# Rounding weights partly on ScalarE and doing the first batch's gated block in seven products, in an attention and SwiGLU kernel

## The chip, the core and the metric

The kernel runs on one core of one Trainium2 chip. The metric is the time of one execution on the device in microseconds (us), as the median of several. A profiled execution gives the span from the first to the last instruction, some 2 us less than that execution's time. A run of one core has no second core to compare with, so it counts as slow only where it is over 1.5% above the fastest of its kernel.

## The reference

Two blocks follow each other. Attention masks a score wherever the six hash bits of query and key differ; its output, put back as 3072 tokens of 512, goes through a gated feed-forward block.

```python
batch, n_heads, seq, head_dim = (4, 8, 768, 64)          # n_tokens 3072, d_model 512, d_ff 1536
q_bits = (np.einsum('bhsd,dk->bhsk', q, proj) > 0)       # k_bits likewise, 6 bits each
scores = np.where(mask, scale * q @ k^T, -1e9)           # mask: equal bits
attn = softmax(scores);  x = (attn @ v) as (3072, 512)
g = x @ w_gate;  silu = g * (1.0 / (1.0 + np.exp(-g)))
val = x @ w_val
return (silu * val @ w_out).astype(np.float32)
```

The three weight matrices are double precision. The kernel sees each double as two 32-bit words, loads them in 36 pieces of 128 x 512 doubles (512 KB each: 12 of gate, 12 of value, 12 of down weights), and rounds every piece to fp32 itself.

## The kernel before

Work on a pair of heads is cut into units: one half of the queries against one sixth of the keys, so 12 units a pair and 48 a batch. A half of a pair (six units) ends in a norm, whose first VectorE instruction is a reciprocal `r`. There is one such `r` for every six units, so its starts serve as a clock for the whole kernel.

The program order on each engine is the order in which this code issues instructions. Attention of batch one runs alone (there is nothing to multiply yet) while VectorE rounds weights. From batch two on, products of the feed-forward block of the batch before are put between the units of attention. Rounding takes seven VectorE operations a piece, in a loop of two buffers:

```python
wraw = ctx.enter_context(tc.tile_pool(name="wraw", bufs=2))
def narrow():
    for i, (w, _) in enumerate(pieces):
        t = words.pop(i)
        lo, hi = t[:, :, 0], t[:, :, 1]
        wi = w.bitcast(I32)
        nc.vector.tensor_scalar(wi, hi, scalar1=3, scalar2=0x3FFFFFFF, ...)       # shift, and
        yield True
        nc.vector.scalar_tensor_tensor(out=wi, in0=hi, scalar=-(1 << 30), ...)    # sign
        yield True
        ...                       # four more: top bits of lo, rounding bit, add, abs of hi
        nc.vector.scalar_tensor_tensor(out=w, in0=hi, scalar=float(897 << 20), in1=w, ...)
        load_words(i + 2)         # refills the buffer just read
        yield True
```

`narrow_on(n)` advances this generator by `n` yields. The feed-forward block of batch one is done with plain products; those of batches two to four with seven block products in place of eight (`up_strassen`, `down_strassen`), which need sums of weight blocks. After batch one's up block, those sums are formed and sent to DRAM, from where they come back group by group:

```python
if b == 0:
    up_plain(x); down_plain(out_of)
else:
    up_strassen(x, b, first); ... down_strassen(out_of)
```

```python
LATE = 2 * NP * 2 * NCH                 # two batches
for u in range(0, LATE, 2):             # two units at a time
    score(u); score(u + 1)              # TensorE scores, then ScalarE exponentials
    for x in left: attend(x)            # TensorE
    while due: norm(due.pop(0))
    for x in left: add(x)               # VectorE: acc, sums of exponentials
    ...
    if not atoms:                       # batch one: nothing to multiply
        narrow_on(3 if u % 12 == 6 else 2)
        continue
    credit += 5.5
    while atoms and credit >= atoms[0][0]:
        size, atom, _ = atoms.pop(0); credit -= size
        atom()                          # a product of the feed-forward block
        narrow_on(2 * size)
for u in range(LATE, N + NCH, NCH):     # batches three and four: six units at a time
    ...                                 # scores, norm, scores, attend, then 15.75 products
```

PSUM has three banks for products and sums, and two double ones for scores.

The softmax here doesn't subtract the row's maximum and nothing guards it: scores larger than these inputs give would overflow.

## Time and profile before

| | before |
|---|---|
| median (three runs) | 1076.83 us |
| profiled span, mean granted TensorE clock | 1073.6 us, 1.000 |
| `r` of batch one's last half | 119.08 us |
| `r` of batch two's last half | 379.98 us |
| that `r` to the end | 693.6 us |

The prediction shows the main lines of this profile. The rows show TensorE's busy share, in tenths, and its granted clock, in tenths of full speed, over 40 slices of the span.

```profile
PE   9999999999999999999999999999999999999998
PEclk9999999999999999999999999999999999999999
```

No slice has an idle TensorE or a lowered clock. The stretch from batch one's last `r` to batch two's last (start:end, length, then busy us and instructions of PE, PEld, DVE, ACT and POOL, granted clock, DMA share, GB/s) says the same of the part that the change rebuilds:

```profile
119.08:379.98 260.90, 257.21 (x998) 125.46 (x998) 223.69 (x377) 58.34 (x88) 41.16 (x68) 1.00 0.41 122
```

TensorE loses 3.7 of 260.9 us there with VectorE at 86%. ScalarE is at 22%, and nothing that it does there concerns the weights.

### The profile page before, as it was taken

The numbers are of one execution on the slowest core, as the hardware profiler recorded it, in microseconds if no ns is written. First come the engines' busy times: TensorE is split into PE (matmuls) and PEld (weight loads), VectorE is DVE, ScalarE is ACT, GpSimd is POOL, SyncE is SP. The second block draws the span as 40 slices with busy tenths as digits, with TensorE's granted clock in tenths as the row PEclk, the third lists the DMA queues.
The fourth block names the chain that finished last, engine by engine and source line by source line (L and its number), as shares of the span: only waits on it lengthen the run. The fifth ranks groups of instructions, "written<-read, shape, count | busy, mean of one in ns | idle before, by whom it ended". The sixth has DMA issues, their size and how long they took to land.

```text
span 1073.6 us, 11817 instructions
## 1 busy us (share of the span) xinstructions
PE 1059.8 (99%) x4537; PEld 589.1 (55%) x4537; DVE 731.9 (68%) x1209; ACT 280.0 (26%) x449; POOL 86.0 (8%) x169
## 2 busy tenths in 40 slices
PE   9999999999999999999999999999999999999998
PEld 4444454554543444455555667554545777555687
DVE  5888988999897564767667465675757554555632
ACT  5544322212222123223232222323333010111100
POOL 1000000000014400010000000000000000111000
PEclk9999999999999999999999999999999999999999
DMA  6333322413325832251512212241212100333101
GB/s 167 75 84 84 84 78 93 109 60 108 92 89 160 296 104 57 66 132 55 113 50 84 50 35 50 69 114 54 80 54 69 54 17 24 103 103 103 35 20 40
DMA packets 110328, 88.86 MB, mean 83 GB/s; under 512 B 86496, under 2 KB 95200, under 8 KB 110272
## 3 DMA queue, kind: packets, MB, share of 16 engines
q0 software_dynamic: 16416, 62.27, 18.5%
q1 hardware_dynamic: 93056, 25.64, 10.9%
q8 instruction: 36, 0.59, 0.2%
q10 hardware_dynamic: 800, 0.20, 0.1%
q14 instruction: 20, 0.16, 0.0%
HBM read 70.78 MB, written 17.30 MB: 82 GB/s over the span
## 4 chain that ended last, share of the span: by engine, by line
PE 92%; DVE 6%; DMA 1%; ACT 1%; issue 0%; ACTq 0%; DVEq 0%
PE up L511 30%; PE po L511 15%; PE sc L422 15%; PE av L433 12%; PE up L493 11%; PE po L614 4%; DVE r L461 2%; PE sum L458 2%; PE hps L360 2%; DVE acc L444 1%; DMA ram<-ws 1%; DVE xT L464 1%; PE hps L372 1%; DVE acc L448 1%; ACT A L424 0%; PE idle L137 0%
## 5 line engine op out<-in xcount | busy, mean ns | idle before, releaser
L511 PE MATMUL up<-xT,wup 128*128 128x384 f32 x576 | 205.5, 490 | 0.0
L422 PE MATMUL sc<-qT,kT 64*128 64x384 f32 x768 | 165.5, 509 | 4.5 <-ACT A L424 1.9
L424 ACT ACTIVATE A<-sc 128x768 f32<-128x768 f32 x160 | 128.9, 812 | 128.6 <-PE sc L422 89.9
L511 PE MATMUL up<-xc,wup 128*128 128x384 f32 x432 | 158.7, 490 | 2.5 <-DVE c L515 1.9
L511 PEld LDWEIGHTS up<-xT,wup 128*128 128x128 f32 x576 | 107.8, 190 | 81.3 <-DVE hid L515 3.9
L461 DVE RECIPROCAL r<-sum 128x384 f32<-128x384 f32 x32 | 81.8, 2558 | 93.4 <-PE sum L458 93.4
L493 PE MATMUL up<-xT,wup 128*128 128x384 f32 x384 | 130.4, 492 | 2.1 <-DVE hid L481 1.0
L448 DVE TENSOR_TENSOR acc<-acc,A 128x768 f32<-128x768 f32 x128 | 121.9, 952 | 3.3
L433 PE MATMUL av<-A,vraw 128*64 128x386 f32 x640 | 117.8, 497 | 0.0
L511 PEld LDWEIGHTS up<-xc,wup 128*128 128x128 f32 x432 | 80.5, 190 | 63.3 <-DVE c L515 9.9
L422 PEld LDWEIGHTS sc<-qT,kT 64*128 64x128 f32 x768 | 63.1, 186 | 78.0 <-issue 43.4
L493 PEld LDWEIGHTS up<-xT,wup 128*128 128x128 f32 x384 | 71.0, 190 | 60.7 <-issue 4.2
L515 DVE TENSOR_TENSOR c<-c,up 128x384 f32<-128x384 f32 x108 | 57.9, 550 | 55.8 <-PE up L511 55.4
L271 POOL DMA_DIRECT2D wup<-ram x72 | 38.6, 536 | 581.6 <-PE up L511 581.5
L515 DVE TENSOR_TENSOR hid<-hid,up 128x384 f32<-128x384 f32 x108 | 57.5, 548 | 39.6 <-PE up L511 39.1
L433 PEld LDWEIGHTS av<-A,vraw 128*64 128x64 f32 x640 | 40.2, 136 | 65.1 <-issue 65.1
L614 PE MATMUL po<-wo,hid 128*128 128x512 f32 x144 | 63.6, 596 | 0.0
L422 PE MATMUL sc<-qb,kb 64*128 64x384 bf16 x384 | 63.2, 323 | 0.0
L476 ACT ACTIVATE c<-up 128x384 f32<-128x384 f32 x42 | 20.6, 490 | 155.1 <-PE up L493 98.8
L511 PE MATMUL po<-wup,hid 128*128 128x256 f32 x216 | 50.0, 381 | 0.0
L511 PE MATMUL po<-wo,hid 128*128 128x256 f32 x216 | 49.7, 379 | 0.0
L511 PE MATMUL po<-wo,wup 128*128 128x256 f32 x216 | 49.6, 379 | 0.0
(108 smaller groups left out, 1002.1 us busy)
## 6 DMA issues: line engine op xcount, KB each, us to landing
wup<-ram POOLq DMA_DIRECT2D x36, 512.0 KB, 3.8
wup<-ram POOLq DMA_DIRECT2D x36, 384.0 KB, 3.4
vraw<-in_v_dram SPq DMA_DIRECT2D x16, 384.0 KB, 3.2
words<-in_moe_w_val_dram POOLq DMA_DIRECT2D x12, 512.0 KB, 3.9
words<-in_moe_w_out_dram POOLq DMA_DIRECT2D x12, 512.0 KB, 3.6
ram<-ws POOLq DMA_DIRECT2D x12, 512.0 KB, 4.6
words<-in_moe_w_gate_dram POOLq DMA_DIRECT2D x10, 512.0 KB, 3.9
qraw<-in_q_dram SPq DMA_DIRECT2D x48, 96.0 KB, 3.5
```

The source lines that it names most:

```text
L271: nc.gpsimd.dma_start(places[k % 2][:, PARTS[part], :], ram[k % NG][:, PARTS[part], :])
L360: nc.tensor.matmul(ps[:, 0:HQ], hash_w[name], T[name, n][:, half * HQ : (half + 1) * HQ], start=True, stop=True)
L422: nc.tensor.matmul(sc[:, h, 0:HQ], x["k", n][rows, ks], x["q", n][rows, qs], start=start, stop=not start)
L424: nc.scalar.activation(weights(u)[:, :, 0:HQ], sc[:, :, 0:HQ], AF.Exp, scale=SCALE)
L433: nc.tensor.matmul(ps[h * D : (h + 1) * D, 0:AW], raws["v", n][:, h, c, :], a[:, h, :], start=c == 0, stop=c == NCH - 1)
L448: nc.vector.tensor_tensor(acc[n, half], acc[n, half], a[:, :, 0:HQ], op=ALU.add)
L458: nc.tensor.matmul(ps[h * D : (h + 1) * D, 0:HQ], ones, t[:, h, :], start=True, stop=True)
L461: nc.vector.reciprocal(r, ps[:, 0:HQ])
L493: nc.tensor.matmul(ps, up_weight(w, f, j), x[j][:, halves[half]], start=j == 0, stop=j == NJ - 1)
L511: nc.tensor.matmul(ps, a, x, start=start and i == 0, stop=i == len(pairs_) - 1, skip_group_check=True)
L515: nc.vector.tensor_tensor(o, a, b, op=op)
L614: nc.tensor.matmul(ps, hidden(f, half)[:, i * P : (i + 1) * P], wo[:, f, :], start=f == 0, stop=f == NF - 1)
```

## The change

The intent is to spend less TensorE time in batch one's feed-forward block, by giving it seven products too. For that the weights must be rounded and their sums formed before batch one's attention ends, which VectorE alone can't do; so three of the operations per piece go to the lightly loaded ScalarE. The core of the diff, with cuts marked:

```diff
     def narrow(i):
+        nc.vector.tensor_single_scalar(w, w, FLOOR, op=ALU.max)
+        ahead = scalar_steps(i + 1)          # ScalarE's three, for the NEXT piece
+        for k in range(3):
+            if ahead:
+                ahead[k]()
             yield True
+            ...                              # VectorE: shift (k == 0), sign (k == 1)
         nc.vector.tensor_tensor(wi, wi, lo, op=ALU.add)
-        ...                                  # four of VectorE's seven are gone or changed
-            load_words(i + 2)
+        load_words(i)
         yield True
+    def scalar_steps(i):
+        return [lambda: nc.scalar.activation(lo.bitcast(FP32), top, AF.Identity, bias=whole, ...),
+                lambda: nc.scalar.activation(lo, lo.bitcast(FP32), AF.Identity, bias=unwhole),
+                lambda: nc.scalar.activation(w, hi.bitcast(FP32), AF.Abs)]
+    EARLY = 16
     def load_words(done, queue=nc.gpsimd):
+        for i in range(len(words), len(pieces)):
+            if i - done > (4 if i < EARLY else 2):
+                break
+            words[i] = (spare[i % 5] if i < EARLY else       # five buffers, in `hid`
+                        wraw.tile([P, PIECE, 2], I32, ...))  # two, from piece 16 on
...
+    def form(n, pair): ...                   # sums of an up group as soon as its pieces are rounded,
+                                             # straight to DRAM
...
-    LATE = 2 * NP * 2 * NCH
+    LATE = NP * 2 * NCH
-        narrow_on(3 if u % 12 == 6 else 2)
+        prepare_on(2 if u < 4 else 4)        # batch one
...
-        credit += 15.75
+        credit += 14 if n < 2 * NP else 15.75
             atom()
-            narrow_on(2 * size)
+            ahead += 1.4 * size
+            prepare_on(int(ahead))
+            ahead %= 1
...
-        if b == 0:
-            up_plain(x)
-            down_plain(out_of)
-        else:
-            up_strassen(x, b, first)
+        up_strassen(x, b, first)
```

The five early buffers lie in the tensor that holds the gated block's output, which is free until batch one's products begin. Batch two moves from the two-unit loop to the six-unit loop. The key's hash bits are now taken by ScalarE, too, with a short VectorE scaling behind.

## The prediction

> **What bounds the kernel now.** I read the busy shares, then the chain of waits, then stretches of time, then single instructions.
>
> ```profile
> PE 1059.8 (99%) x4537; PEld 589.1 (55%) x4537; DVE 731.9 (68%) x1209; ACT 280.0 (26%) x449; POOL 86.0 (8%) x169
> ...
> PE 92%; DVE 6%; DMA 1%; ACT 1%; issue 0%; ACTq 0%; DVEq 0%
> ```
>
> TensorE is busy for 99% of the span and is 92% of the chain that ended last. Removing matmul time therefore shortens the run one for one, unless a second engine is nearly full where it is removed. Stretches (start:end, length, then busy time of PE, PEld, DVE, ACT, POOL) show where that is so:
>
> ```profile
> 78.00:104.00 26.00, 25.36 (x150) 11.25 (x148) 23.10 (x31) 12.71 (x21) 1.06 (x2) 1.00 0.31 74
> 125.00:165.00 40.00, 40.00 (x162) 20.45 (x163) 36.04 (x61) 10.20 (x16) 3.17 (x6) 1.00 0.37 90
> 478.82:508.43 29.61, 29.61 (x131) 14.96 (x130) 20.14 (x32) 10.42 (x18) 2.15 (x4) 1.00 0.21 63
> 508.43:537.19 28.76, 28.76 (x123) 14.80 (x122) 19.10 (x30) 8.14 (x14) 2.14 (x4) 1.00 0.48 105
> ```
>
> While the weights are rounded (first two rows) VectorE is at 89 to 90%; later (last two) at 67%. So the early stage has two bounds almost level. Its chain shows VectorE in the loop: reciprocal, xT, acc, then the exponential that frees the next scores:
>
> ```profile
> 106.70 2.56 DVE r L461
> ...
> 109.32 0.62 DVE xT L464
> 109.94 0.88 DVE acc L444
> ...
> 110.92 0.82 ACT A L424
> ...
> 111.79 1.89 PE sc L422 x12
> ```
>
> The chain also gives the pace of each product (two records per matmul):
>
> ```profile
> 232.27 7.94 PE up L493 x24
> 368.10 7.92 PE po L614 x18
> 702.54 27.46 PE up L511 x84
> 865.91 18.33 PE po L511 x84
> ```
>
> Plain up: 7.94/12 = 0.662 us a matmul; plain down 7.92/9 = 0.88; seven-product up 27.46/42 = 0.654; seven-product down 18.33/42 = 0.436.
>
> **What the Trainium skill says.** "VectorE: DVE Perf Modes", "The perf-mode tier table", puts fp32 tensor_scalar at twice the rate of tensor_tensor. The trace agrees: 128x512 takes 421 ns as a tensor_scalar and 690 as a two-tensor form, so the two-source steps are the costly ones. "ScalarE: Activation LUTs", "What ACT_TABLE_LOAD costs", gives an ACTIVATE 186 ns + 0.833 ns per element and about 93 more for a pointer bias; the trace's 384-element sign with a pointer bias took 580 ns against 600. My estimate from it for the new 512-element ones is 0.71, 0.71 and 0.61 us, about 1.8 a piece when they overlap. "PSUM — Partial Sum Buffer", "Engine vs sequencer instructions", calls the ScalarE and VectorE queues strict FIFO: an instruction that waits holds up everything behind it. No line of this trace isolates that, but my third step rests on it. "DMA: Bandwidth & Descriptors", "Anatomy of one DMA — SWDGE (gpsimd) path", gives 2.0 us + bytes/436e3, 3.2 us for a 512 KB piece; here it is 3.6 to 3.9.
>
> **The change, part by part.**
>
> *TensorE.* Batch one's up block: 192 plain matmuls (127.1 us) become 12 x 7 x 2 = 168 (109.9): -17.2. Its down block: 72 x 0.88 = 63.4 becomes 126 x 0.436 = 54.9: -8.5. Pairs 5 to 7 hash with 32-column blocks instead of 0.745 us full matmuls: about -4 in all. Steps of six units switch less between products, and the wait on stores of the sums (7 times, 15.4 us of VectorE idle, PE only 48.44 of 50 us busy at 300 to 350 us) goes. I take the total from spans. In the old kernel the reciprocal of batch one's last half starts at 119.08 and that of batch two's last half at 379.98: 260.9 us. The new stage is eight steps of 14 units, as in the last two rows above: 4 x (29.61 + 28.76) = 233.5. The old rest (1073.6 - 379.98 = 693.6) still holds 27 plain down matmuls (23.8); the new has one chunk of 42 (18.3): 688.1. With nothing stretched: 119.1 + 233.5 + 688.1 = 1040.7, or -33.
>
> *First batch (attention alone), VectorE.* The period is 26.2 us per pair of heads (reciprocals 80.47 to 106.70). Old VectorE load per pair, by distances between starts: ten acc at about 0.95, two norms of 3.15, two bit evictions of 0.61, 13 rounding steps of 0.57: 24.4. New: acc and norms 15.8; one stage of weights, i.e. four pieces of four steps (0.455 + 0.455 + 0.61 + 0.69 = 2.2; max is single-source) = 8.8, and eight 128x256 sums at 0.4 = 3.2; two bf16 scalings of the key bits, estimated at 0.2 each. That is 28.2: VectorE becomes the bound. The first pair absorbs it, because VectorE idles 6.35 us at 20 to 27 us; the other three stretch by 2.2, 2.2 and 0.6 (the last has only half the sums), with some jitter: **+5.4**. ScalarE rises from 12.8 to about 21 of 28 us per pair; its words come four ahead, so I expect no stall from it.
>
> *Second batch, first six steps (84 product steps of TensorE, 29.2 us each step).* VectorE: 18.7 per step (last two rows above, less four evictions of 0.667 us that move to ScalarE), plus 1.4 x 14 = 19.6 preparation steps of about 0.5 = 9.9. That is 28.6 of 29.2, 98%, and not evenly spread: some 22 us of it falls in the 18.3 us of the products, while in the 10.9 us of scores it waits for sums. Three PSUM banks let it lag two or three products. Worked through by hand, counting from the end of a gate group's fifth product: VectorE, 0.8 late, frees the first bank at 2.2 us where TensorE could use it at 1.3 (0.9 lost); in the value group the same bank comes free at 11.5, wanted at 10.5 + 0.9 (0.1). About 1.1 us a step.
>
> *The same steps, ScalarE.* From piece 16 on, a piece's words are asked for two ahead only, after the last VectorE instruction of the piece that held the buffer. The instruction order puts the first ScalarE step on those words just behind the next max. The load takes about 0.5 + 3.8 us, one piece lasts 4/1.4 products = 3.7 us. So ScalarE stands at its queue's head waiting for the load, and the copy of p1 and the tanh behind it come late, and VectorE and the PSUM banks after them. The hand working again, for a step that only rounds, counting from its first scores: loads asked for at 10.8, 18.1 and 25.3 us land at 14.6, 21.8 and 29.0; the last holds the max of its piece to 30.8, the second holds a tanh to 22.9, and the last product ends at 31.3 where it would end at 29.2 alone; the next reciprocal is another 0.3 late. That is 2.4 in place of 1.1. Taking it for all six: 2.4 x 6 = **+14.4**.
>
> *Sum.* 1040.7 + 5.4 + 14.4 = 1060.5 of span; the timed median lies 3.2 over the profiled span (1076.83 - 1073.6): 1063.7. My hand working ignores that the rate 1.4 and the 14 units were surely chosen by someone who measured, so I shade it down to **1061 us**.
>
> **Rivals.**
> - *Pure TensorE gain*: stalls absorbed, about 1040.7 + 3.2 = 1044. For it: at 125 to 165 us TensorE lost nothing with VectorE at 90%. Against: the load sums of 28.2 against 26.2 and 28.6 against 29.2.
> - *VectorE or the load loop bounds the second batch fully*: 4 to 6 us per step, 1070 to 1083. For it: the arithmetic of 4.3 against 3.7 us. Against: the scores part of each step breaks the loop, and eight of the 20 preparation steps in steps two and three are sums that need no words.
> - *Bringing batch one's weights back from DRAM is late*: 12 more groups of 0.9 MB in about 175 us is some 60 GB/s over the 90 to 105 now, with loads of 3.4 to 3.8 us that have over 13 us of slack. I give it no time.
>
> **Range and chances.** The two stretches are the uncertainty: 1 to 10 us in the first, 4 to 27 in the second. That gives 1046 to 1075. Two per cent faster is 1055.3, some 6 us under my figure: chance 0.3. Slower by 2% needs 1098: 0.02. The rest, 0.68, is within 2%.
>
> **What would show it.** The 264 plain matmuls vanish, the seven-product ones rise from 504 + 378 to 672 + 504, and each keeps its pace. The reciprocal of batch one's last half comes at about 124.5, and VectorE is over 95% busy from 40 to 120 us. The six steps from there last about 31.6 each with ScalarE idle on "DMA words" and TensorE idle on VectorE; the later steps stay at 29. I am wrong if the six steps last 29 (then about 1047), if ScalarE delays exponentials in the first batch, or if VectorE's new instructions take other times than I gave them.

## The result, and the profile after

Ratios here are the mean time of one kernel's fast runs over that of the other's of the same rounds, so they are not quite the ratio of the medians quoted beside them.

| | before | after |
|---|---|---|
| median | 1076.82 us | 1104.47 us (1102.44 to 1105.51) |
| ratio, 95% interval | | 1.0256, 1.0238 to 1.0273 |
| profiled span, clock | 1073.6 us, 1.000 | 1103.7 us, 0.985 |
| `r` of batch one's last half | 119.08 | 128.04 |
| `r` of batch two's sixth step | | 358.30 |
| `r` of batch two's last half | 379.98 | 416.50 |
| that `r` to the end | 693.6 | 687.2 |

The changed kernel is 2.6% slower; 1061 us and the whole range were wrong. The page after, with the busy line, the slices and the chain of waits:

```profile
PE 1049.9 (95%) x4597; PEld 601.9 (55%) x4597; DVE 714.1 (65%) x1230; ACT 387.1 (35%) x629; POOL 99.5 (9%) x192
...
PE   8999888888888999999999999999999999999998
...
PEclk9999898999999999999999999999999999999999
...
PE 76%; DVE 13%; ACT 4%; DMA 4%; issue 3%; POOL 0%; DVEq 0%; POOLq 0%; ACTq 0%
```

TensorE's share of the chain fell from 92 to 76%, VectorE's rose from 6 to 13%, and ScalarE and DMA have 4% each. The loss has a place: from the fifth slice to the thirteenth TensorE is at 8 tenths, that is from some 110 to 359 us (a slice is 1103.7/40 = 27.6 us), and the clock falls below nine tenths in two of these slices. After that both rows are as before. So are the paces of the products, here in the chain:

```profile
547.24 27.50 PE up L535 x84
...
867.81 18.33 PE po L535 x84
```

Before, 84 records of the same two kinds took 27.46 and 18.33 us. The stretches, from one `r` to the next, first a pair of batch one and then the six steps of batch two:

```profile
71.35:99.66 28.31, 26.07 (x150) 11.12 (x148) 27.33 (x43) 21.56 (x35) 8.95 (x14) 1.00 0.73 221
```

```profile
128.04:166.91 38.87, 33.02 (x120) 16.11 (x120) 31.60 (x57) 14.33 (x23) 4.51 (x8) 0.90 0.47 126
166.91:203.85 36.94, 33.24 (x128) 15.68 (x128) 27.58 (x52) 16.62 (x27) 7.95 (x13) 0.91 0.42 135
203.85:240.85 37.00, 31.14 (x120) 15.18 (x120) 27.04 (x49) 14.07 (x22) 8.07 (x13) 0.95 0.60 173
240.85:281.59 40.74, 33.50 (x128) 15.87 (x128) 28.78 (x52) 22.74 (x36) 4.77 (x9) 0.92 0.33 108
281.59:325.18 43.59, 33.34 (x122) 15.76 (x124) 28.55 (x50) 19.73 (x31) 4.25 (x8) 0.92 0.48 129
325.18:358.30 33.12, 30.32 (x130) 14.79 (x132) 27.17 (x47) 12.81 (x21) 2.30 (x6) 1.00 0.19 56
```

In the first batch VectorE is busy for 27.33 of 28.31 us, just as told. The six steps take 230.3 us together where the prediction had 189.5. VectorE is at 66 to 82% in them, so its average does not bound them; TensorE has 35.7 us of idle time (230.3 less the sum 194.6 of its busy column) and is itself slower, at a clock of 0.90 to 0.95 in the first five. Who waits for what, from 128 to 359 us (engine, line, what it waited for: us in total, times, longest):

```profile
ACT words L270 <- DMA words<-in_moe_w_out_dram: 36.7, 8, 9.6
...
PE up L535 <- ACT hid L594: 13.0, 5, 3.8
...
ACT words L270 <- DMA words<-in_moe_w_val_dram: 11.8, 3, 5.2
...
PE sc L467 <- ACT room L469: 11.0, 4, 3.7
...
PE up L535 <- DVE c L539: 8.0, 9, 1.5
```

L270 is the first of the three ScalarE steps. With 7.5 us more on the gate weights it waits 56.0 us for words. And TensorE waits for ScalarE: for the copy of a product (L594) and for the exponential that frees a score bank (L469), 24.0 us together. Its waits for VectorE come to 11.7 us (the 8.0 for a product's bank, 2.5 for the last additions of a step, and 1.2 in two more). One such place in full, ScalarE's and then TensorE's instructions (start, duration, engine, line, what; in brackets the idle time before it and what ended it):

```profile
204.59 0.75 ACT L270 ACTIVATE words<-words,columns 128x512 f32<-128x512 uint16 x1 [3.46 <-DMA words<-in_moe_w_val_dram]
205.37 0.75 ACT L272 ACTIVATE words<-words,columns 128x512 int32<-128x512 f32 x1
206.02 0.64 ACT L273 ACTIVATE room<-words 128x512 f32<-128x512 f32 x1
206.69 1.51 ACT L469 ACTIVATE room<-sc 128x768 f32<-128x768 f32 x2
```

```profile
202.99 0.81 PE L503 MATMUL sum<-acc,ones 128*64 128x384 f32 x4
207.55 1.65 PE L467 MATMUL sc<-qT,kT 64*128 64x384 f32 x4 [3.74 <-ACT room L469]
```

The scores were ready at about 200.4 us (the last two score records started at 200.09). Their exponentials stand in ScalarE's queue behind three rounding steps, whose words were asked for at 200.60 and came at about 204.5. So the exponentials start at 206.69, six microseconds late, and TensorE idles for 3.74. Then it pays again: the four score records after the gap take 1.65 us where 0.81 is usual, until about 211 us. That is half pace, and it is how waits turn into a lowered clock here. Seven stretches of granted clock 0.50 start between 128 and 359 us, six of 3.41 us and one of 6.83, each inside an idle time of TensorE of 2.54 to 3.77 us or at most 1.3 us after it. Three of these idle times ended with a copy of ScalarE's, three with its exponentials, one with VectorE.

The requests for words were not held up in GpSimd's queue, from which they are issued: from piece 18 on they start 0.5 to 0.9 us after VectorE's last operation on the piece that held the buffer, one of the 18 excepted (2.1).

### The profile page after: what moved, and what is told of

It reads as the page before. It is cut to its first block, busy times and chain, and to the rows that moved or that the text cites. A ratio compares the mean times of both kernels' runs of the same rounds, so it can differ in the third digit from the quotient of the medians.

```text
span 1103.7 us, 12215 instructions
## 1 busy us (share of the span) xinstructions
PE 1049.9 (95%) x4597; PEld 601.9 (55%) x4597; DVE 714.1 (65%) x1230; ACT 387.1 (35%) x629; POOL 99.5 (9%) x192
## 4 chain that ended last, share of the span: by engine, by line
PE 76%; DVE 13%; ACT 4%; DMA 4%; issue 3%; POOL 0%; DVEq 0%; POOLq 0%; ACTq 0%
PE up L535 32%; PE po L535 20%; PE sc L467 12%; PE av L478 9%; DVE acc L493 3%; DMA words<-in_moe_w_out_dram 2%; DVE r L506 2%; PE sum L503 1%; DVE room L334 1%; DVE room L304 1%; DVE room L302 1%; ACT kb L398 1%; PE hps L415 1%; ACT words L270 1%; DMA words<-in_moe_w_val_dram 1%
## 5 line engine op out<-in xcount | busy, mean ns | idle before, releaser
L535 PE MATMUL up<-xT,room 128*128 128x384 f32 x768 | 279.4, 495 | 16.2 <-ACT hid L594 14.3
L535 PE MATMUL up<-xc,room 128*128 128x384 f32 x576 | 214.3, 495 | 8.0 <-DVE c L539 6.5
L535 PEld LDWEIGHTS up<-xT,room 128*128 128x128 f32 x768 | 143.4, 191 | 130.3 <-ACT hid L594 19.1
L535 PEld LDWEIGHTS up<-xc,room 128*128 128x128 f32 x576 | 108.3, 192 | 92.2 <-DVE c L539 18.9
L469 ACT ACTIVATE A<-sc 128x768 f32<-128x768 f32 x144 | 114.7, 810 | 95.1 <-PE sc L467 75.8
L493 DVE TENSOR_TENSOR acc<-acc,A 128x768 f32<-128x768 f32 x128 | 121.9, 953 | 2.7 <-DVE acc L489 0.5
L319 POOL DMA_DIRECT2D room<-ram x96 | 52.3, 545 | 725.8 <-PE up L535 717.6
L467 PEld LDWEIGHTS sc<-qT,kT 64*128 64x128 f32 x768 | 64.5, 190 | 94.5 <-issue 33.6
L521 ACT ACTIVATE th<-c 128x384 f32<-128x384 f32 x72 | 37.6, 522 | 86.2 <-DVE c L522 49.7
L535 PE MATMUL po<-room,hid 128*128 128x256 f32 x288 | 67.0, 382 | 0.0
L535 PE MATMUL po<-wo,room 128*128 128x256 f32 x288 | 66.1, 379 | 0.0
L535 PEld LDWEIGHTS po<-room,hid 128*128 128x128 f32 x288 | 54.0, 190 | 11.6 <-issue 2.0
L535 PEld LDWEIGHTS po<-wo,hid 128*128 128x128 f32 x288 | 54.6, 190 | 8.6 <-issue 1.3
```

Of the source, the lines that this page charges most:

```text
L319: nc.gpsimd.dma_start(places[k % 2][:, PARTS[go], :], ram[k % NG][:, PARTS[go], :])
L467: nc.tensor.matmul(sc[:, h, 0:HQ], x["k", n][rows, ks], x["q", n][rows, qs], start=start, stop=not start)
L469: nc.scalar.activation(weights(u)[:, :, 0:HQ], sc[:, :, 0:HQ], AF.Exp, scale=SCALE)
L493: nc.vector.tensor_tensor(acc[n, half], acc[n, half], a[:, :, 0:HQ], op=ALU.add)
L521: nc.scalar.activation(th, g, AF.Tanh, scale=0.5)
L535: nc.tensor.matmul(ps, a, x, start=start and i == 0, stop=i == len(pairs_) - 1, skip_group_check=True)
```

## The experiments

My theory after the result: the load loop of two buffers leaves ScalarE waiting at the head of its queue, and what stands behind it, exponentials above all, stalls TensorE, which then also loses clock. The rivals: VectorE's own load in the steps of six units; the six-unit steps as such; and ScalarE's longer busy time. Fourteen kernels ran, each in three rounds beside the kernel before. "Six steps" is the time from batch one's last `r` to the sixth after it.

| run | median us | ratio (95%) | last `r`, batch one | six steps |
|---|---|---|---|---|
| (the change) | 1104.47 | 1.0256 (1.0238 to 1.0273) | 128.04 | 230.3 |
| e1_third | 1077.80 | 1.0017 (1.0002 to 1.0031) | 128.13 | 201.7 |
| e2_noround | 1059.67 | 0.9846 (0.9829 to 0.9862) | 128.22 | 184.4 |
| e3_vector | 1118.14 | 1.0389 (1.0373 to 1.0404) | 150.30 | 220.6 |
| e4_actlate | 1084.96 | 1.0075 (1.0053 to 1.0098) | 126.78 | 211.1 |
| e5_two | 1124.01 | 1.0433 (1.0416 to 1.0451) | not used | not used |
| e6_oldact | 1166.94 | 1.0843 (1.0827 to 1.0859) | 144.09 | |
| e7_two_third | 1077.54 | 1.0009 (0.9994 to 1.0024) | 127.59 | |
| e8_three | 1085.51 | 1.0082 (1.0065 to 1.0099) | 121.59 | |
| e9_oldact_late | 1079.21 | 1.0027 (1.0012 to 1.0042) | 119.01 | |
| e10_pool | 1081.42 | 1.0050 (1.0034 to 1.0067) | 133.01 | |
| e11_pool2 | 1076.80 | 1.0013 (0.9996 to 1.0029) | 135.60 | |
| e12_noscalar | 1075.86 | 1.0001 (0.9983 to 1.0019) | 127.16 | 200.5 |
| e13_novector | 1061.62 | 0.9867 (0.9849 to 0.9884) | 128.09 | 186.4 |
| e14_third_late | 1080.37 | 1.0035 (1.0019 to 1.0051) | 127.15 | 206.3 |

e2, e12 and e13 give wrong results on purpose; e8 gives a wrong result that was not intended. The others were correct. A first form of e5 was a deadlock of the schedule, since a group of products held all three PSUM banks when a sum wanted one, and a first form of e12 put NaN into the weights; both were mended.

### e1_third: a third buffer for the words

The changed kernel, with 4 KB a partition that lay unused between two other buffers as a third one, and words asked for three pieces ahead.

```diff
-            if i - done > (4 if i < EARLY else 2):
+            if i - done > (4 if i < EARLY else 3):
-            words[i] = (spare[i % 5] if i < EARLY else
+            words[i] = (spare[i % 5] if i < EARLY else third if i % 3 == 0 else
```

> The changed kernel with a third buffer for the raw words of pieces 16 to 35 (in 4 KB of the shared area that nothing uses), so that each load is asked for three pieces ahead in place of two; arithmetic and order of all other instructions as they are. Theory A (the load loop: ScalarE stands at the head of its queue for a load asked for only just before, and p1 copies, tanh and exponentials wait behind it): the waits of ScalarE on DMA words fall from 56 us to under 15, the six steps of batch two fall from about 38 us to 30 to 32 us, the clock goes back to 1.00, and the time to 1060 to 1070. Theory B (VectorE is simply overloaded in batch two, and the load wait only fills time that would be lost anyway): steps stay at 36 to 38 and the time at 1095 to 1105.

The median fell from 1104.5 to 1077.8 us. The six steps fell from 230.3 to 201.7, by 28.6 us, which is the whole gain of the span (1103.7 to 1075.2). The two longest, the fourth and fifth, are now 34.00 and 31.90:

```profile
230.77:264.77 34.00, 30.59 (x130) 14.71 (x132) 28.55 (x52) 22.98 (x36) 4.77 (x9) 1.00 0.36 118
264.77:296.67 31.90, 29.50 (x122) 14.63 (x124) 28.16 (x49) 16.91 (x26) 3.72 (x7) 1.00 0.62 171
```

The work of ScalarE and VectorE is the same: over the six steps they are busy for 100.3 and 170.7 us after the change and for 101.6 and 169.8 here. The waits went, and the clock is back at 1.00 from the third step on (0.92 and 0.98 in the first two). The place shown above reads:

```profile
194.36 0.77 ACT L274 ACTIVATE words<-words,columns 128x512 f32<-128x512 uint16 x1 [0.94 <-DMA words<-in_moe_w_val_dram]
...
196.53 1.51 ACT L473 ACTIVATE room<-sc 128x768 f32<-128x768 f32 x2
```

ScalarE waits 0.94 in place of 3.46 us, and in all 6.9 in place of 56.0. Summed over the six steps TensorE's busy time is 183.6 in place of 194.6 us and its idle time 18.1 in place of 35.7. So of the 28.6 us, 17.6 are idle time and 11.0 the same products at a lower granted clock. TensorE's waits for ScalarE's exponentials are gone (11.0 us before) and those for its copies fell from 13.0 to 5.3, but those for VectorE stay, 12.6 us in place of 11.7:

```profile
PE up L539 <- DVE c L543: 7.3, 8, 1.5
...
PE sum L507 <- DVE acc L497: 3.9, 1, 3.9
```

The load loop is thus a cause, and its size is shown. It is not the only one: the stage still takes 26.6 us more than the 175.1 (six eighths of 233.5) that the prediction gave it without stretching, and theory A's ranges of 1060 to 1070 us and 30 to 32 us a step were missed (33.6 a step).

### e2_noround: no rounding from piece 16 on

```diff
+        if i >= EARLY:
+            nc.gpsimd.dma_start(pieces[i][0]..., v[0, 0:2]...)   # any numbers, so that the tile is written
+            for _ in range(4): yield True
+            return
```

> Wrong results on purpose: pieces 16 to 35 are not rounded, a DMA copies other fp32 data (v) straight into their place; sums, stores to DRAM, products and all of the first batch as in the changed kernel. A and B alike: all stalls of batch two go, VectorE has 10 us less per step, steps of 29 us; my accounting of TensorE gives 1040.7 + 8.4 (first batch, as measured) + 3 = 1052. If it stays above 1065, bringing weights back from DRAM or the seven products themselves cost what I did not count.

1059.7 us, 1.5% faster than before, where I had expected 1052. The six steps take 184.4 us, and the fifth is a step as the prediction had it:

```profile
250.91:279.54 28.63, 28.63 (x122) 14.88 (x124) 19.40 (x30) 8.24 (x13) 5.07 (x8) 1.00 0.64 143
```

The distance to 175.1 that is left, 9.3 us, is therefore not rounding. 3.9 of it lie in the sixth step (33.12 us in this run and in the change alike, against 29.2), where nine sums for the down weights and the hashing of the next pair meet; the rest is in the first four steps.

### e3_vector: the old seven VectorE operations in the new structure

```diff
-        nc.vector.tensor_single_scalar(w, w, FLOOR, op=ALU.max)
-        ahead = scalar_steps(i + 1)
+        ...                                  # the seven VectorE operations of before, four yields
```

> Undoes the ScalarE part alone: all seven rounding operations on VectorE again (1.8 us more VectorE per piece), same buffers, loads, order of pieces and steps. Theory A: ScalarE is free and never waits for words, but VectorE is the bound: 35 us per pair in the first batch (28.3 now) and about 38 per step in batch two, so about 1125 to 1135. Theory B: steps grow by the full 9 us of VectorE on top of 38, to 46, and the time passes 1165.

1118.1 us, slower than the change by 13.7 (in other rounds). Batch one's last `r` comes at 150.30, some 22 us later, since VectorE now bounds that batch by itself, and the six steps are 9.7 us shorter, though VectorE is busy for 203.3 us in them in place of 170.7. So giving part of the rounding to ScalarE paid in the first batch and cost in the second. (The time lies under both theories' ranges, 1125 to 1135 and over 1165.) Whether ScalarE's instructions as such cost anything is left to e12.

### e4_actlate: ScalarE's steps as late as they can go

The steps on the next piece's words are issued later in the program order, two of them behind the next load request, so that less of ScalarE's work stands behind a wait.

```diff
-            if ahead:
-                ahead[k]()
+            if ahead and k == 2:
+                ahead[0]()
...
         load_words(i)
+        for step in ahead[1:]:
+            step()
```

> Two buffers as in the changed kernel, but the three ScalarE steps of a piece stand later in the order: the first with the third VectorE step of the piece before, the other two after its last, so that a load has some 2 us more before ScalarE comes to it. VectorE waits longer for its own input. Theory A, in the form that it is the instructions behind the waiting ScalarE step that cost: 1080 to 1092. Theory A, in the form that the round trip load, ScalarE, VectorE is what costs: 1100 to 1110. Theory B: 1104 or more.

1085.0 us: 19.5 of the third buffer's 26.7 us, from the order of instructions alone. ScalarE's waits for words are 28.8 in place of 56.0 us, and the six steps take 211.1. This is a second proof of the load loop that adds no memory and takes no work away.

### e5_two and e7_two_third: batch two in steps of two units again

e5 keeps everything of the change but the six-unit steps; e7 is e5 with the third buffer of e1.

```diff
-    LATE = NP * 2 * NCH
+    LATE = 2 * NP * 2 * NCH
...
+        credit += 14 / 3
+        while atoms and credit >= atoms[0][0]:
+            ...
+            ahead += 1.4 * size
+            prepare_on(int(ahead))
```

> Undoes the six-unit steps of batch two alone: two units and 4.67 products in turn, as the old kernel had it, all else as in the changed kernel (two buffers, ScalarE rounding, seven products for batch one). Theory A: the same rounding is now spread over the scores too, a piece lasts about 6 us in place of 3.7, which is more than the 4.5 us of a load, so ScalarE waits little: batch two takes 240 to 250 us in place of 288 and the time is 1055 to 1068. If the time stays above 1085, the waits for loads do not come from the crowding of the rounding into the product part of a step.

> Two-unit iterations in batch two as in e5_two, with the third buffer of e1_third as well. Theory A: a little better than e5_two (0 to 6 us), since the third buffer only helps where loads still hold ScalarE; about 1053 to 1062, which would beat both kernels. If it equals e5_two, the spreading alone had ended the waits; if it is above 1070, VectorE's sum of work (28.6 of 29.2 us per six units) bounds batch two whatever the order.

Both were misses (1055 to 1068 and 1053 to 1062 us were expected). I had thought the six-unit steps part of the trouble, and in e5 going back to two units made it worse: 1121.7 to 1124.6 us in the three fast runs. Its profiled run (1795.1 us at a clock of 0.556) is not used, so how it loses is not shown. With the third buffer, two units (1077.5) and six (1077.8) are level, and the third buffer is worth 46.5 us in two-unit steps against 26.7 in six-unit ones. But TensorE does not lose its time in the same places. These are all its waits in e7 from 127 to 333 us that the view lists:

```profile
PE sc L471 <- ACT qb L402: 12.5, 3, 4.4
...
PE up L539 <- DVE xc L543: 4.7, 1, 4.7
```

The waits for VectorE to free a product's bank, 7.3 us in e1, are gone; in their place scores wait for hash bits that ScalarE takes (L402), which stand in its queue among tanh, copies and rounding steps. So the level times do not show that the length of the steps costs nothing; one cost took the place of another. That in two-unit steps exponentials come more often behind a waiting step is my reading, argued and not shown.

### e6_oldact and e9_oldact_late: ScalarE's steps in the kernel before

The kernel before, with the change's rounding and nothing else of it. In e6 the three steps for the next piece follow VectorE's first operations; in e9 the same three steps are issued about five slots after the request for their words, two of them behind the next request.

```diff
+            ahead = scalar_steps(i + 1)
+            nc.vector.tensor_single_scalar(w, w, 2.0**-15, op=ALU.max)
+            if ahead:
+                ahead[0]()               # e9: only at the third VectorE operation
             ...
+            if ahead:
+                ahead[1]()               # and ahead[2]; e9: after load_words(i + 2)
```

> The kernel before with the ScalarE part alone: three of seven rounding steps of a piece on ScalarE, the first of them standing right behind the request for its load (two buffers), the same pace of pieces. Theory A (an engine that meets a load at the head of its queue holds up what stands behind): slower than before although VectorE has 1.8 us less per piece, 1079 to 1095. If relief of VectorE is all that counts: 1070 to 1077.

> e6_oldact (the kernel before with the ScalarE part) with the ScalarE steps later in the order: the first one five VectorE step slots behind the request for its load in place of one, some 4 us. Nothing else moves; VectorE and ScalarE do the same work. If the 91 us of e6_oldact come from ScalarE standing at a load, most of them go: 1080 to 1105. If they come from the ScalarE work as such (1.8 us a piece in the way of exponentials and tanh), the time stays at 1150 or more.

e6 takes 1166.9 us, 8.4% more than before and far above the 1079 to 1095 expected; e9 takes 1079.2, 0.3% more. The two do the same work, and 87.7 us lie between them. The waits of e6 over the whole run, and one of e9:

```profile
DVE c L494 <- ACT c L493: 84.4, 23, 6.0
...
ACT words L228 <- DMA words<-in_moe_w_val_dram: 61.8, 10, 10.0
ACT words L228 <- DMA words<-in_moe_w_out_dram: 61.4, 10, 10.9
```

```profile
ACT words L228 <- DMA words<-in_moe_w_out_dram: 27.5, 8, 6.0
```

In e6 VectorE waits 84.4 us for the tanh (L493) that stands behind the rounding steps. In e9 ScalarE still waits 55.5 us for words in all (27.5 with 19.3 and 8.7 on the other two), about as long as in the change, and yet the whole is only 3 us slower than before (VectorE's relief, some 1.8 us a piece, included). So the sum of ScalarE's idle time is not the price; the price is what stands behind it in the queue and who needs that. This pair, the same work in another order, is the cleanest proof of the mechanism, and it says that the trouble needs neither the seven products nor the six-unit steps.

### e8_three: three preparation steps an iteration in batch one

e7 with `prepare_on(2 if u < 4 else 3)`, so that VectorE is not the bound in batch one.

> e7_two_third with three preparation steps per iteration of the first batch in place of four: VectorE falls there from 28.3 us per pair to about 25.5, under TensorE's 26.2, so the last reciprocal of batch one should come at about 119 to 121 in place of 128, if it is VectorE's sum of work that stretches the first batch. Some 22 preparation steps (11 us of VectorE) move to batch two, which is at its limit: I expect that to eat most or all of the gain, net -4 to +6 us against e7_two_third.

The result was wrong, which I had not foreseen: with fewer steps in batch one, words of the early pieces still lie in the tensor that batch one's products write, and the program order lets them be overwritten (argued from a count of the steps, not tested). As a timing it says this much: the period of a pair is back at 26.2 us and batch one's last `r` comes at 121.59, 6.0 earlier than in e7, yet the whole takes 8.0 us longer (-4 to +6 was expected). The work that leaves batch one costs more in batch two.

### e10_pool and e11_pool2: the sums of up weights on GpSimd

e1 with the sums that go to DRAM on GpSimd; e11 with the steps spread otherwise (`4 + (u % 4 == 0)` in batch one, 1.2 a product later).

```diff
-            nc.vector.tensor_tensor(o, x, y, op=op)
+            nc.gpsimd.tensor_tensor(o, x, y, op=op)
```

> e1_third with the 48 sums of the upper weights on GpSimd (9% busy) in place of VectorE. VectorE loses 3.2 us per pair in the first batch and about 3 us in each of steps 1 to 3. If VectorE's sum of work stretches the first batch, the period there goes from 28.3 to 26.2 to 26.6 and the last reciprocal of batch one to 120 to 122 (128.1 in e1_third); with 5 to 8 us from batch two the time is 1060 to 1067, faster than both kernels. If GpSimd's sums disturb VectorE or hold up the loads that GpSimd issues, 1075 or more.

> e10_pool with more of the rounding in the first batch (4.5 steps per iteration in place of 4) and so a lower rate in batch two (1.2 per product in place of 1.4), as the room that GpSimd makes on VectorE allows: period of the first batch about 26.3 to 27, steps of batch two about 1.3 us shorter. Between 1052 and 1064; if the first batch gets as much longer as batch two gets shorter, equal to e10_pool.

e10 is a miss: 1081.4 us, 3.6 slower than e1, and batch one got longer (last `r` at 133.01) though VectorE had less to do. GpSimd takes 1043 ns for a sum of 128 x 256, where VectorE takes 418, and VectorE's additions got slower beside it, as did its max over 128 x 512 (428 ns in e1, 511 here). By groups (busy us, mean ns of one), after the change (e1's mean is 954) and in e10:

```profile
L493 DVE TENSOR_TENSOR acc<-acc,A 128x768 f32<-128x768 f32 x128 | 121.9, 953 | 2.7 <-DVE acc L489 0.5
```

```profile
L497 DVE TENSOR_TENSOR acc<-acc,A 128x768 f32<-128x768 f32 x128 | 128.7, 1006 | 2.7
```

e11 made up for that by moving steps, and at 1076.8 us is level with before, where 1052 to 1064, or a time equal to e10's, was expected. Neither is a gain.

### e12_noscalar and e13_novector: which engine's rounding the rest is

Both are e1 with one half of the rounding gone from piece 16 on: e12 without ScalarE's three steps, e13 without VectorE's four.

```diff
-        if i == len(pieces):              # e12: scalar_steps
+        if i >= EARLY:
             return []
...
+        if i >= EARLY:                    # e13: narrow, ScalarE's steps and the loads alone
+            ahead = scalar_steps(i + 1)
+            for k in range(4):
+                if ahead and k < 3: ahead[k]()
+                if k == 3: load_words(i)
+                yield True
+            return
```

> Wrong results on purpose: e1_third without the three ScalarE steps of pieces 16 to 35 (a DMA puts other data in the place of their result; the last VectorE step is an and in place of an add, so that nothing becomes infinite). VectorE works as in e1_third. If VectorE's sum of work (28.3 us busy per step in e1_third) is what is left: 1071 to 1077. If ScalarE's steps in the way are: 1060 to 1065.

> Wrong results on purpose: e1_third without the four VectorE steps of pieces 16 to 35, ScalarE's three steps kept. If VectorE's sum is what is left: 1060 to 1064. If ScalarE's steps in the way are: 1068 to 1077.

e12 is 1075.9 us and its six steps 200.5, 1.1 under e1 (before rounding to tenths). e13 is 1061.6 us and its six steps 186.4, 15.2 under e1. With a third buffer, ScalarE's steps cost next to nothing, and what is left of the rounding is VectorE's four operations.

### e14_third_late: both cures

e1 with the order of e4.

> e1_third with the later place of the ScalarE steps of e4_actlate. The rest of the load waits (7 us in e1_third) goes, but VectorE now waits for ScalarE at the start of each piece, about 1 us: 1072 to 1080. Under 1070 would mean that the place of the ScalarE steps, not the work, was what was left.

1080.4 us (ratio 1.0035, in other rounds than e1's 1.0017). The two cures do not add; with the words there in time, later ScalarE steps are no help.

No kernel with right results beat the one before. e1, e7 and e11 are correct and level with it within 0.2%.

## Why the prediction was wrong

On record were 1060.5 us of span before the shading. The span was 1103.7, so 43.2 us were missed. By the prediction's own stretches they lie here: up to batch one's last `r` 3.5 (128.04 against 124.5); the six steps 40.8 (230.3 against 189.5, its 175.1 and 14.4); the last two steps of batch two -0.2 (58.2 against 58.4); the rest -0.9 (687.2 against 688.1).

*TensorE.* Right. The plain products are gone, 672 and 504 seven-product matmuls took their place at the old pace, and both later stretches came out within 1 us. The gain of about 33 us is there; it is spent earlier.

*First batch, VectorE.* The mechanism was right. The period of 28.2 was measured at 28.31 and 28.32 us, with VectorE at 97% from 43 to 100 us. Two smaller terms were mis-sized. The first pair did not absorb its share: its second `r` came at 42.95 where it had been at 40.38, 2.6 us later. And the last pair was stretched by 2.2 us, not 0.6: at its end TensorE waits 3.63 us for the last additions, and the sum and the scores behind run at half pace:

```profile
126.45 1.55 PE L503 MATMUL sum<-acc,ones 128*64 128x384 f32 x4 [3.63 <-DVE acc L493]
127.93 1.65 PE L467 MATMUL sc<-qT,kT 64*128 64x384 f32 x4
```

Of the instruction times, max (0.42 us) and the sums (0.418) were as worked out; the scalings of key bits took 0.31, not 0.2.

*The same steps, ScalarE.* This is the step that failed. It said "So ScalarE stands at its queue's head waiting for the load, and the copy of p1 and the tanh behind it come late", which the waits, e1, e4, e6 and e9 show. But it ended in "That is 2.4 in place of 1.1. Taking it for all six: 2.4 x 6 = **+14.4**", of which 7.8 us were the load loop's (1.3 a step). The third buffer is worth 28.6. For the copies, which it followed, the size was near: TensorE's waits for them are 7.7 us less in e1. The hand working left out two things. It did not follow a waiting ScalarE to the exponentials of the next step's scores, where TensorE has nothing else to do: four waits, 11.0 us, the 3.74 above among them. And it took TensorE's pace as fixed, while each longer idle time was followed by 3.4 us or more at half clock: 11.0 of the 28.6 us.

*Second batch, first six steps, VectorE.* Mis-sized, too: 1.1 us a step, 6.6 in all. Without the load loop the six steps still exceed 175.1 by 26.6 us: 17.2 between e1 and e2 for the rounding, nearly all of it VectorE's (15.2 by e13), and 9.3 for the sums and the new order. VectorE was busy for 28.3 us a step in e1, as the 28.6 had it, which is 84% of that stage. In the kernel before it was busy for 86% of batch two, and TensorE lost 3.7 us there against 18.1 in e1's six steps. In e1 TensorE pays for VectorE in two places: at the banks of products (7.3 us in eight waits) and at the last additions of the first step, one wait of 3.92 us with half clock behind it. Without VectorE's rounding (e13) the second is gone and the first is 2.7. In e7, with the work spread over two-unit steps, both are gone, which speaks for its uneven placing within the step; e7 is no faster all the same, with 12.5 us of waits for hash bits. A kernel with neither was not built, so this stays argued.

*The rivals.* The second, "VectorE or the load loop bounds the second batch fully", was nearest, but gave 4 to 6 us a step; the six steps exceed 175.1 by 55.2, that is 9.2 a step. The pure TensorE gain did not occur even without any rounding from piece 16 on (e2: 1059.7). Bringing batch one's weights back from DRAM was not late, as told: the loads take 3.4 to 3.9 us as before, and no wait of TensorE is on them.

*Range and chances.* The stretch of batch two was given 4 to 27 us and took 55. The two causes came side by side (in the change TensorE waits 24.0 us for ScalarE and 11.7 for VectorE), where the rival had them as one or the other. Two sums are off: the stretches as given make 1049 to 1081, not 1046 to 1075, and the first batch's 2.2 a pair should be 2.0 (28.2 less 26.2), measured 2.1. The 3.2 us of median over span set two different executions against each other; the profiled one took 1.8 more than its span. None of this explains the miss. The shading down, on the ground that someone had surely measured the rate of 1.4, had no line of a profile behind it. And 0.02 for slower was far too sure: a queue that waits for a load at its head was the one part of the change whose cost no line of the profile before could show.

## What to carry to other kernels

Moving work to a lightly loaded engine is not safe just because the engine has time: if the work begins with a wait for a load, everything behind it in that queue waits too, so count buffers against the longest load and put the first reader of a load well behind its request. Judge such a wait by what stands behind it, not by its length (taking away 49 of 56 us of waiting gained 28.6 here; with 55.5 us in another order a kernel was 3 us slower). A cure for one engine's waits leaves the other's in place, so list TensorE's waits by engine before and after. And price an idle time of TensorE with the slower products that follow: in the change half clock followed every one of 2.54 us and more.

## What the Trainium skill lacked or had wrong

- The cost of a waiting head of queue: "PSUM — Partial Sum Buffer", "Engine vs sequencer instructions", calls the queues strict FIFO, with which these runs agree (the exponentials that started at 206.69 us, behind three rounding steps), but no page that I read says what it can cost. Here it was 28.6 us of 1103.7 (third buffer), and 87.7 us between e6 and e9, which differ in issue order alone.
- "TensorE: Matmul & The Clock Gate", "HAM oscillation — how this bites in real kernels", gives the rule of no idle gaps over about 3.4 us. Keeping under that length was not enough here. After gaps of 3.63 and 3.74 us four score records took 1.65 in place of 0.81 us, but in the change half clock also followed gaps of 2.54, 3.04, 3.09 and 3.27 us, and in e9 one of 2.12, while none followed gaps of 2.59 (e4) and 3.10 us (e3). What decides between these is not shown, and the lengths are approximate, since the ends of matmuls are modelled. What the page lacks for a kernel like this one is that a wait of ScalarE for a load leads to it: 11.0 us of slower products over six steps.
- "ScalarE: Activation LUTs", "What ACT_TABLE_LOAD costs", is some 0.06 us low for the rounding steps, which read strided words: 512 elements with a pointer bias took 0.77 us where its formula gives 0.71, and without one 0.67 where it gives 0.61.
